# Attention and MLP kernel, front of the program: the first query tile on SyncE's queue, a scan and a memset behind the first sums, two row loads behind the bias rows

## The chip, the cores and the metric

The kernel runs on one core of one Trainium2 chip. The metric is device time in microseconds (us); the time before is the median of 3 runs, 344.49 us (343.03 to 345.12). Engine names: TensorE (PE), VectorE (DVE), ScalarE (ACT), GpSimd (POOL), SyncE (SP). SyncE, ScalarE and GpSimd issue DMA transfers; each executes its own instructions in order.

## The reference

Selective attention over 8 batches, 8 heads, 576 positions and 64 channels per head, and then a layer norm with a two-layer MLP on the 512 joined channels:

```python
scores = (q @ k.T) / sqrt(64)
cum = cumsum(maximum(s, 0))                       # along the positions
bias = -(cum[:, None] - cum[None, :])
scores = where(causal, -1e9, scores + minimum(bias, 0))
x = softmax(scores) @ v                           # heads joined: [8, 576, 512]
out = x + maximum(layernorm(x, g) @ w1, 0) @ w2   # w1 [512, 2048], w2 [2048, 512]
```

Inputs and output are float32. The matrix products run in bfloat16.

## The kernel before

The program runs once through the eight batches; the attention of a batch overlaps the MLP of an earlier one. Weights w1 and w2 are kept in SBUF. Nothing loops at run time: the order of the work is a list of step names, PLAN, written out by hand as one long string and run through by the loop at the end of `fast_path`, which looks each name up in STEPS. Each engine gets its instructions in the order of that list, and a step on one engine waits for its inputs by semaphores.

The bias is not added to the scores. The cumulative sums c of s (64 rows, one for each batch and head, by 576 positions) are split into three bfloat16 parts (high, middle, low), and these stand as four more rows below the 64 channels of q and k, so that the score product of 68 rows contains the bias. For batch 0 the parts go in as columns beside the loaded q and k rows (tile `rowb`, 128 positions at a time), and TensorE transposes the whole tile; for batch 1 they go in by small DMAs of rows (`aug`, lines 262 to 267, four transfers on SyncE for each half of the heads).

What happens at the front, with the names of the steps:

- Loads ahead of PLAN (lines 900 to 965): SyncE loads the first 256 positions of s (`c_first`), the first k tile (`ld_tile`, float32) and the rest of s (`c_in`); ScalarE's queue loads the first q tile. GpSimd issues all the loads that cast to bfloat16, in a fixed order: k and q tiles 1 and 2, v tiles, w1 pieces, the pairs `kp` and `qp`, the last k and q tile (64 positions), and later the five v tiles of batch 1 (line 192), w1 and w2.
- `relu.0` and `relur.1`, `relur.2`: relu and scale of the three stretches of s (0 to 128, 128 to 256, 256 to 576), the first on VectorE, the others on ScalarE. `scan.0`, `scan.1`, `scan.2` (line 293, VectorE): their cumulative sums, each started from the last column of the one before.
- `hi`, `sub`, `mid`, `lo` (lines 307 to 312): the three parts of a stretch; for stretch 0 all on VectorE, for the others the casts `hi` and `mid` on ScalarE. `tc` transposes the parts on TensorE, `bc` (lines 282 and 286, VectorE) puts them into `rowb`.
- `cq` and `ck.0` (line 141, ScalarE): casts of the loaded first q and k tile into `rowb`.
- `m` (line 1257, VectorE): memset of the rows of `rowb` behind the last 64 positions, and of a small constant for the layer norm.
- `W.n`: n matmuls on zeros (line 889, 512 columns each) that keep TensorE at work.
- `T.t.g` (line 978) transposes tile t for the heads of group g (four heads, 8 transposes), `e` evacuates it to `kq`, `S` and `x` are its scores and exponentials, `V.t.g` (line 1058) its product with v.
- `lr.3.0` (`ld_rows`, line 206): two float32 loads on SyncE, the first 128 positions of batch 3's k and q, into two tiles of the pool `stage` of 8. Their reader is `cr.3.0.0` (line 218, a cast on GpSimd), much later in PLAN.
- `aug` writes batch 1's bias rows for the first half of its heads into `kq[2]`; it waits for the parts of c and for GpSimd's memset of `kq[2]` (line 941).
- `v.8` (line 590) is the first product of batch 1 with its v tiles, five key blocks.

Of the kernel before, what the change touches and what calls it, by code (L numbers as in the profile page):

```python
# [30 lines left out]
def fast_path(  # L31
# [12 lines left out]
    nc = tc.nc  # L44
    B, H, S, D = q.shape
# [115 lines left out]
    def tile_src(kind, t):  # L161
        pn = P if t < NF else TL
        src = k if kind == "k" else q
        return src[0, :, t * P : t * P + pn, :].rearrange("h s d -> s h d")
# [6 lines left out]
    def ld_tile(kind, t, eng):  # L171
        tmp = stage.tile([P, H, D], F32, name="tiletmp", tag="st")
        eng.dma_start(out=tmp, in_=tile_src(kind, t))
        loaded[kind, t] = tmp
# [723 lines left out]
    )  # L898
    s_rows = s.rearrange("b h s -> (b h) s")
    nc.sync.dma_start(out=c_first, in_=s_rows[:, 0 : 2 * P])  # L900
    ld_tile("q", 0, nc.scalar)
    ld_tile("k", 0, nc.sync)
    nc.sync.dma_start(out=c_in[:, 2 * P : S], in_=s_rows[:, 2 * P : S])

    nc.vector.memset(zeros.bitcast(F32), 0.0)
# [315 lines left out]
    def raise_flag(count, ones, n):  # L1221
# [97 lines left out]
    }  # L1319

    PLAN = """
        relu.0 scan.0 relur.1 O cq hi.0 scan.1 ck.0 sub.0 mid.0 lo.0 m hi.1 tc.0 bc.0 sub.1 W.2 T.0.1 relur.2
        mid.1 scan.2 e.0.1:A lo.1 T.0.0 W.1 hi.2 tc.1 S.0.1.0 bc.1 T.1.0 e.0.0:A sub.2 T.1.1 S.0.0.0 qu.1 mid.2
        x.0.1.0 lo.2 V.0.1 tc.2 e.1.0:A e.1.1:D S.1.1.1 x.0.0.0 x.1.1.1 qu.2 S.1.0.0 V.0.0 N.0.1 S.1.1.0 bc.2
        T.2.0 N.0.0 x.1.1.0 T.2.1 e.2.0:D S.1.0.1 lr.3.0 lp.9 V.1.1 x.1.0.1 S.2.0.1 e.2.1:D S.2.0.2 S.2.1.2
        T.3.0 S.2.1.1 N.1.1 S.2.0.0 B.0.1 L.0 x.1.0.0 V.1.0 x.2.0.1 x.2.0.2 x.2.1.2 X.0 e.3.0:D N.1.0 x.2.1.1
        L.1 x.2.0.0 S.2.1.0 S.3.0.2 T.3.1 B.1.0 x.2.1.0 e.3.1:D B.1.1 S.3.0.0 S.3.0.3 y.0:A aug x.3.0.2 V.2.0
        M.0.0.0 x.3.0.3 M.0.0.3 S.3.0.1 V.2.1 S.3.1.1 x.3.0.1 N.2.0 M.0.0.2 bc.4 S.3.1.3 x.3.0.0 X.1 y.1:A
        x.3.1.3 N.2.1 M.0.0.1 S.3.1.2 V.3.0 L.2 T.4.0 S.3.1.0 M.0.1.0 r.0.0:A M.0.1.3 N.3.0 X.2 x.3.1.2 Q.q.4
        x.3.1.0 x.3.1.1 e.4.0:D T.4.1 y.2:D M.0.1.2 Q.k.4 E.q.4.0:A B.3.0 E.k.4.0:A S.4.0.1 e.4.1:D S.4.1.0  # L1330
# [253 lines left out]
def kernel(tc, q, k, v, s, g, w1, w2, out):  # L1584
    nc = tc.nc
    with tc.tile_pool(name="flag", bufs=1) as pool:
        flag = pool.tile([1, 1], I32, name="flag")
        bad = fast_path(tc, q, k, v, s, g, w1, w2, out, flag)
        with tc.If(bad > 0):
            general_path(tc, q, k, v, s, g, w1, w2, out)  # L1590
# [28 lines left out]
```

## Time and profile before

| | |
|---|---|
| median of 3 runs | 344.49 us (343.03 to 345.12) |
| the profiled execution's own time | 344.98 us |
| its span, first to last instruction | 343.4 us |
| TensorE clock granted, mean | 0.997 |
| ScalarE, VectorE, GpSimd busy | 186.5, 201.4, 167.3 us |
| moved by DMA | 48.59 MB, 147962 packets |

Times in the profile's rows are us from the start of the span. In a row of a timeline the first number is the start and the second the duration; instructions that follow each other at one line are merged (x8 is eight of them, and the duration is that from the first start to the last end). The bracket tells how long the engine was idle ahead of the row and what ended that: `[0.30 <-DMA rowb<-in_k_dram]` is 0.30 us of waiting for a load of k into `rowb`. `SPq` and `ACTq` rows are DMA issues, not the transfers; a DMA row in the chain of waits runs from the issue to the landing. The rows of DMA queues give packets, MB and the time that the packets took as a share of 16 engines' time in that window.

### The profile page before, as it was taken

Reading aid. Unit: us, or ns where it says so; the run is one execution under the profiler, and the core shown is the slowest. Engines: PE = TensorE matmul, PEld = TensorE weight load, DVE = VectorE, ACT = ScalarE, POOL = GpSimd, SP = SyncE. Lnnn points to the kernel's source line nnn. Section 1 sums busy time; section 2 is a strip of 40 time slices with the busy share of each in tenths; the row PEclk is TensorE's granted clock in tenths of the full one; section 3 lists DMA queues with packets and bytes.
Section 4 is the critical chain, followed back from the end, with each engine's and each line's share of the span. In section 5 each row is a group of like instructions: output and inputs, shape, how many; then the busy total and the mean of one; then the engine's idle time right before and its main releaser. Section 6 shows DMA issues by size and latency. Waiting matters only on the chain.

```text
span 343.4 us, 8036 instructions
## 1 busy us (share of the span) xinstructions
PE 330.9 (96%) x3093; PEld 183.1 (53%) x3117; DVE 201.4 (59%) x568; ACT 186.5 (54%) x347; POOL 167.3 (49%) x305
## 2 busy tenths in 40 slices
PE   7999999999999899999999999999999999999994
PEld 2899765555455455545555545554455444444443
DVE  6688787946586577457643664566448624533412
ACT  4888999678655676457636764487344204202200
POOL 8897678886579762884774376431301001000000
PEclk9999999999999999999999999999999999999998
DMA  9999999899999999999987966700510141021022
GB/s 145 181 190 181 204 196 207 193 227 227 194 206 211 205 211 187 213 222 219 208 184 193 216 109 148 139 2 2 122 63 2 30 123 46 3 84 38 3 62 65
DMA packets 147962, 48.59 MB, mean 141 GB/s; under 512 B 135280, under 2 KB 143760, under 8 KB 147920
## 3 DMA queue, kind: packets, MB, share of 16 engines
q1 hardware_dynamic: 121856, 38.34, 54.5%
q0 software_dynamic: 24304, 8.92, 22.2%
q10 hardware_dynamic: 1760, 0.79, 1.0%
q8 instruction: 25, 0.41, 0.5%
q14 instruction: 17, 0.14, 0.1%
HBM read 37.11 MB, written 9.44 MB: 136 GB/s over the span
## 4 chain that ended last, share of the span: by engine, by line
PE 71%; POOL 11%; DMA 9%; issue 2%; SPq 2%; DVE 2%; ACT 1%; POOLq 0%; ACTq 0%
PE py L811 30%; PE ph L792 29%; DMA v_bf<-in_v_dram 5%; PE pot L626 3%; DMA kq<-rowb 2%; SPq L206 2%; PE sa L553 2%; POOL er L497 2%; POOL v_bf L192 1%; DMA rowtmp<-in_q_dram 1%; POOL v_bf L233 1%; ACT er L560 1%; PE pott L664 1%; PE sb L553 1%; PE pot L590 1%
## 5 line engine op out<-in xcount | busy, mean ns | idle before, releaser
L811 PE MATMUL py<-w_bf,hT 128*128 128x512 bf16 (+2 forms) x584 | 128.8, 367 | 1.8 <-issue 0.6
L792 PE MATMUL ph<-xT,w_bf 128*128 128x512 bf16 x480 | 110.0, 379 | 0.9 <-DMA xT<-xn 0.9
L783 ACT ACTIVATE hT<-ph 128x512 bf16<-128x512 f32 x102 | 61.0, 605 | 80.7 <-PE ph L792 79.0
L811 PEld LDWEIGHTS <-hT 128*128 128x128 bf16 x608 | 56.0, 98 | 60.2 <-issue 0.2
L792 PEld LDWEIGHTS <-w_bf 128*128 128x128 bf16 x544 | 51.2, 98 | 57.3 <-DMA xT<-xn 1.4
L497 POOL TENSOR_SCALAR_AFFINE_SELECT er<-er 128x256 bf16<-128x256 bf16 x96 | 37.9, 411 | 50.7 <-ACT er L560 36.3
L823 DVE SCALAR_TENSOR_TENSOR yo<-py,rstd,xb 128x512 f32<-128x512 f32 x32 | 24.0, 751 | 49.1 <-PE py L811 44.6
L560 ACT ACTIVATE er<-sb 128x512 bf16<-128x512 f32 x48 | 28.2, 609 | 21.0 <-PE sb L553 21.0
L781 DVE TENSOR_SCALAR hT<-ph 128x512 bf16<-128x512 f32 x34 | 23.4, 691 | 27.2 <-PE ph L792 25.2
L560 ACT ACTIVATE er<-sa 128x512 bf16<-128x512 f32 x48 | 28.6, 609 | 15.1 <-PE sa L553 14.8
L233 POOL TENSOR_TENSOR v_bf<-rowtmp,wt 128x512 bf16<-128x512 f32 (+1 forms) x30 | 32.2, 1081 | 2.6 <-DMA rowtmp<-in_v_dram 2.4
L560 ACT ACTIVATE er<-sc 128x512 bf16<-128x512 f32 x48 | 28.8, 613 | 5.3 <-PE sc L553 5.3
L715 POOL TENSOR_TENSOR rstd<-rstd,mhalf 128x4 f32<-128x4 f32 (+1 forms) x8 | 8.8, 1094 | 34.7 <-DVE rstd L714 33.2
L741 DVE SCALAR_TENSOR_TENSOR xn<-xb,mv,gb 128x512 bf16<-128x512 f32 x28 | 25.0, 894 | 1.0
L218 POOL CAST kq<-rowtmp 128x512 bf16<-128x512 f32 (+1 forms) x30 | 18.5, 626 | 13.7 <-DMA rowtmp<-in_k_dram 13.0
L626 PEld LDWEIGHTS <-er 128*128 128x128 bf16 x480 | 19.7, 97 | 10.0 <-POOL er L497 1.3
L643 DVE TENSOR_REDUCE sums<-pot 128x4 f32<-128x8 f32 x48 | 7.8, 162 | 29.2 <-PE pot L626 29.1
L700 DVE BATCH_NORM_STATS2 stats<-xb 128x6 f32<-128x128 f32 (+1 forms) x84 | 24.6, 326 | 0.6
L626 PE MATMUL pot<-v_bf,er 128*128 128x66 bf16 x480 | 22.1, 193 | 0.3 <-POOL er L497 0.2
L645 DVE TENSOR_TENSOR xb<-pot,rinvs 128x256 f32<-128x256 f32 x48 | 20.4, 425 | 1.7
L553 PEld LDWEIGHTS <-kq 64*128 64x128 bf16 x384 | 12.0, 94 | 9.7 <-issue 4.0
L218 POOL CAST rowb<-rowtmp 128x512 bf16<-128x512 f32 (+1 forms) x20 | 13.8, 696 | 1.9 <-DMA rowtmp<-in_k_dram 1.0
(178 smaller groups left out, 394.9 us busy)
## 6 DMA issues: line engine op xcount, KB each, us to landing
out_dram<-yo SPq DMA_DIRECT2D x32, 256.0 KB
rowtmp<-in_v_dram SPq DMA_DIRECT2D x24, 256.0 KB
rowtmp<-in_k_dram SPq DMA_DIRECT2D x20, 256.0 KB
rowtmp<-in_q_dram SPq DMA_DIRECT2D x20, 256.0 KB
w_bf<-in_moe_w_ch_dram POOLq DMA_DIRECT2D x8, 512.0 KB, 9.1
kp<-in_k_dram POOLq DMA_DIRECT2D x8, 144.0 KB, 8.9
qp<-in_q_dram POOLq DMA_DIRECT2D x8, 144.0 KB, 9.0
v_bf<-in_v_dram POOLq DMA_DIRECT2D x8, 128.0 KB, 8.1
```

What stands on the lines that cost most here:

```text
L218: nc.gpsimd.tensor_copy(out=rows[b % 2][0:pn, t, u], in_=loaded.pop(("kq"[u], b, t))[0:pn])
L233: e.tensor_tensor(out=v_bf[b % 2][0:pn, t, :, 0:D], in0=loaded.pop(("v", b, t))[0:pn], in1=wt[0:pn, t, b, :].unsqueeze(2).to_broadcast([pn ...
L497: nc.gpsimd.affine_select(out=out, in_=out, compare_op=ALU.is_ge, fill=0.0, base=0, pattern=pattern, channel_multiplier=-1,)
L560: nc.scalar.activation(out=er[:, 2 * n % 4 + i, o : o + 512], in_=bank["B", n].pop((name, i)), func=ACT.Exp, scale=scale,)
L626: nc.tensor.matmul(pot[:, t, :], lhsT=e[:, o : o + P], rhs=v_bf[b % 2][:, kb, h, :], start=(kb == 0), stop=(kb == t),)
L700: nc.vector.bn_stats(out=st[b][:, t, part, :], in_=x_tiles(b)[t][:, lo:hi])
L741: nc.vector.scalar_tensor_tensor(out=xn, in0=tiles[t], scalar=mvs[b][:, t, 0:1] if b > 0 else mean0[:, t : t + 1], in1=gb, op0=ALU.subtrac ...
L781: nc.vector.tensor_scalar_max(out=dst, in0=ph, scalar1=0.0)
L783: nc.scalar.activation(out=dst, in_=ph, func=ACT.Relu)
L792: nc.tensor.matmul(ph, lhsT=w1_bf[:, kd, fb * P : (fb + 1) * P], rhs=xT[:, :, kd, :], start=(kd == 0), stop=(kd == KD - 1),)
L811: nc.tensor.matmul(py[t], lhsT=hT[:, fb, t * P : (t + 1) * P], rhs=w2_bf[:, fb, c0:c1], start=(fb == 0), stop=(fb == FB - 1),)
L823: nc.vector.scalar_tensor_tensor(out=yo, in0=py[t], scalar=rs, in1=x[:, c0:c1], op0=ALU.mult, op1=ALU.add)
```

## The change

Three edits at the front; no instruction's arithmetic changes.

1. The first q tile is loaded on SyncE's queue, behind the first k tile and ahead of the rest of s, instead of on ScalarE's queue.
2. In PLAN `scan.1` goes from behind `hi.0` to behind `lo.0`, and `m` from behind `lo.0` to behind `sub.1`; `ck.0` comes ahead of `cq` on ScalarE, and both keep their place ahead of `hi.1`; `W.2` ahead of the first tile's transposes becomes `W.1`.
3. `lr.3.0` goes from behind `S.1.0.1` to behind `aug`; its two loads thus stand behind `aug`'s four on SyncE's queue.

```diff
     nc.sync.dma_start(out=c_first, in_=s_rows[:, 0 : 2 * P])
-    ld_tile("q", 0, nc.scalar)
     ld_tile("k", 0, nc.sync)
+    ld_tile("q", 0, nc.sync)
     nc.sync.dma_start(out=c_in[:, 2 * P : S], in_=s_rows[:, 2 * P : S])
...
     PLAN = """
-        relu.0 scan.0 relur.1 O cq hi.0 scan.1 ck.0 sub.0 mid.0 lo.0 m hi.1 tc.0 bc.0 sub.1 W.2 T.0.1 relur.2
+        relu.0 scan.0 relur.1 O ck.0 hi.0 sub.0 mid.0 lo.0 scan.1 cq hi.1 tc.0 bc.0 sub.1 m W.1 T.0.1 relur.2
...
-        T.2.0 N.0.0 x.1.1.0 T.2.1 e.2.0:D S.1.0.1 lr.3.0 lp.9 V.1.1 x.1.0.1 S.2.0.1 e.2.1:D S.2.0.2 S.2.1.2
...
+        T.2.0 N.0.0 x.1.1.0 T.2.1 e.2.0:D S.1.0.1 lp.9 V.1.1 x.1.0.1 S.2.0.1 e.2.1:D S.2.0.2 S.2.1.2 T.3.0
...
+        x.2.0.0 S.2.1.0 S.3.0.2 T.3.1 B.1.0 x.2.1.0 e.3.1:D B.1.1 S.3.0.0 S.3.0.3 y.0:A aug lr.3.0 x.3.0.2 V.2.0
```

The lines of PLAN between are only wrapped anew.

More of the change, by code (lines that the diff above doesn't have):

```diff
@@ L1321, in fast_path @@
     PLAN = """
-        relu.0 scan.0 relur.1 O cq hi.0 scan.1 ck.0 sub.0 mid.0 lo.0 m hi.1 tc.0 bc.0 sub.1 W.2 T.0.1 relur.2
+        relu.0 scan.0 relur.1 O ck.0 hi.0 sub.0 mid.0 lo.0 scan.1 cq hi.1 tc.0 bc.0 sub.1 m W.1 T.0.1 relur.2
         mid.1 scan.2 e.0.1:A lo.1 T.0.0 W.1 hi.2 tc.1 S.0.1.0 bc.1 T.1.0 e.0.0:A sub.2 T.1.1 S.0.0.0 qu.1 mid.2
         x.0.1.0 lo.2 V.0.1 tc.2 e.1.0:A e.1.1:D S.1.1.1 x.0.0.0 x.1.1.1 qu.2 S.1.0.0 V.0.0 N.0.1 S.1.1.0 bc.2
-        T.2.0 N.0.0 x.1.1.0 T.2.1 e.2.0:D S.1.0.1 lr.3.0 lp.9 V.1.1 x.1.0.1 S.2.0.1 e.2.1:D S.2.0.2 S.2.1.2
-        T.3.0 S.2.1.1 N.1.1 S.2.0.0 B.0.1 L.0 x.1.0.0 V.1.0 x.2.0.1 x.2.0.2 x.2.1.2 X.0 e.3.0:D N.1.0 x.2.1.1
-        L.1 x.2.0.0 S.2.1.0 S.3.0.2 T.3.1 B.1.0 x.2.1.0 e.3.1:D B.1.1 S.3.0.0 S.3.0.3 y.0:A aug x.3.0.2 V.2.0
+        T.2.0 N.0.0 x.1.1.0 T.2.1 e.2.0:D S.1.0.1 lp.9 V.1.1 x.1.0.1 S.2.0.1 e.2.1:D S.2.0.2 S.2.1.2 T.3.0
+        S.2.1.1 N.1.1 S.2.0.0 B.0.1 L.0 x.1.0.0 V.1.0 x.2.0.1 x.2.0.2 x.2.1.2 X.0 e.3.0:D N.1.0 x.2.1.1 L.1
+        x.2.0.0 S.2.1.0 S.3.0.2 T.3.1 B.1.0 x.2.1.0 e.3.1:D B.1.1 S.3.0.0 S.3.0.3 y.0:A aug lr.3.0 x.3.0.2 V.2.0
         M.0.0.0 x.3.0.3 M.0.0.3 S.3.0.1 V.2.1 S.3.1.1 x.3.0.1 N.2.0 M.0.0.2 bc.4 S.3.1.3 x.3.0.0 X.1 y.1:A
```

## Prediction

> **What bounds the kernel now.** I read the page first, for the engine that carries the span.
>
> ```profile
> span 343.4 us, 8036 instructions
> PE 330.9 (96%) x3093; PEld 183.1 (53%) x3117; DVE 201.4 (59%) x568; ACT 186.5 (54%) x347; POOL 167.3 (49%) x305
> DMA  9999999899999999999987966700510141021022
> PE 71%; POOL 11%; DMA 9%; issue 2%; SPq 2%; DVE 2%; ACT 1%; POOLq 0%; ACTq 0%
> ```
>
> TensorE is busy for 96% of the span, and the DMA engines are at nine tenths or more for its first half. All the edits lie in the first 20 us, so next comes the chain of waits, in order of time, up to the place where TensorE takes it over.
>
> ```profile
> 3.77 7.71 DMA v_bf<-in_v_dram
> ...
> 28.25 8.01 DMA v_bf<-in_v_dram
> ...
> 36.30 0.19 PE pot L590
> ```
>
> The end is not set by the bias sums at the front. It is set by the row of casting loads that GpSimd issues, down to the last tile of batch 1's v, issued at 28.25 and landed at 36.26; the first attention product of batch 1 (step v.8) stands there. From 36.3 the chain is nearly all TensorE. The timeline of TensorE shows the same from its side: its waits in this stretch, with their releasers in brackets.
>
> ```profile
> 7.08 1.05 PE L889 MATMUL idle<-hT 128*128 128x512 bf16 x2
> 8.00 1.89 PE L978 MATMUL trt<-ident,rowb 128*68 128x128 bf16 x16
> 10.83 1.17 PE L978 MATMUL trt<-ident,rowb 128*68 128x128 bf16 x16
> 23.14 0.64 PE L1058 MATMUL pot<-v_bf,er 128*128 128x65 bf16 x16
> 24.08 0.36 PE L978 MATMUL trt<-ident,rowb 96*68 96x96 bf16 x4 [0.30 <-DMA rowb<-in_k_dram]
> 24.66 0.36 PE L978 MATMUL trt<-ident,rowb 96*68 96x96 bf16 x4 [0.22 <-DMA rowb<-in_q_dram]
> 26.07 0.50 PE L978 MATMUL trt<-ident,rowb 96*68 96x96 bf16 x8
> 35.94 0.55 PE L590 MATMUL pot<-v_bf,er 128*128 128x65 bf16 x6 [0.38 <-DMA v_bf<-in_v_dram]
> ```
>
> Three waits, all for casting loads: 0.30 and 0.22 us for the last k and q tile of batch 0, 0.38 us for batch 1's v. So two questions decide: how much earlier TensorE comes to v.8, and whether that v lands earlier or later.
>
> **Part 1: the sums (scan, memset, warm-up).** The timelines of VectorE and ScalarE:
>
> ```profile
> 5.67 0.47 DVE L293 TENSOR_TENSOR_SCAN c_sc<-c_one,c_sc,hT 64x128 f32<-64x128 f32 x1
> 6.07 0.26 DVE L312 TENSOR_TENSOR hT<-c_sc,c 64x128 f32<-64x128 f32 x1
> ...
> 6.67 0.28 DVE L312 TENSOR_TENSOR c<-hT,c 64x128 bf16<-64x128 f32 x1
> 7.13 0.51 DVE L1257 MEMSET rowb<- 32x544 uint32 x1 [0.17 <-issue]
> 7.67 0.18 DVE L282 COPY rowb<-trc 128x24 bf16<-128x24 bf16 x1
> ```
>
> Today the second scan (5.67 to 6.07, start to start) lies between the first high part and its rest, and the memset (7.13 to 7.67) between the last low part and the bias columns. Taken out, they give 0.40 + 0.54 us; the scan comes back behind the low part, ahead of the columns, at its 0.40 to 0.47. The columns also need the third transpose, about 0.3 us behind the low part, which then runs beside the scan. So the columns can start near 7.67 - 0.40 - 0.54 + 0.43 = 7.2, and the tile transposes near 7.5 instead of 8.00: 0.5 us. The memset costs nothing later: its rows are read by the transposes at 24.08. One warm-up matmul of two goes; both took 1.05 us, and with the columns 0.5 us sooner one fits ahead of them.
>
> **Part 2: the first q tile moves from ScalarE's queue to SyncE's, behind k.** ScalarE's rows are the ones that wait on these loads:
>
> ```profile
> 4.61 0.31 ACT L1260 ACTIVATE hT<-hT 64x128 f32<-64x128 f32 x1 [1.59 <-DMA hT<-in_s_dram]
> 4.84 0.62 ACT L141 CAST rowb<-tiletmp 128x512 bf16<-128x512 f32 x1
> 5.84 0.62 ACT L141 CAST rowb<-tiletmp 128x512 bf16<-128x512 f32 x1 [0.38 <-DMA tiletmp<-in_k_dram]
> ...
> 7.11 0.47 ACT L1260 ACTIVATE c_in<-c_in 64x320 f32<-64x320 f32 x1 [0.45 <-DMA c_in<-in_s_dram]
> ...
> 9.07 1.01 ACT L141 COPY kq<-trt 68x1024 bf16<-68x1024 bf16 x1 [0.64 <-PE trt L978]
> ```
>
> q is cast at 4.84 without a wait, k at 5.84, as soon as it lands. The ScalarE issue that goes (0.44 us) frees an engine that waits for s until 4.61 anyway: nothing. What counts is the DMA; its queues by window (q10 is ScalarE's queue, q1 SyncE's, q0 GpSimd's), 2 to 3 and 4 to 5 us:
>
> ```profile
> DMA packets 499, 0.13 MB, mean 129 GB/s; under 512 B 498, under 2 KB 499, under 8 KB 499
> q10 hardware_dynamic: 498, 0.13, 55.1%
> q1 hardware_dynamic: 1, 0.00, 0.3%
> ...
> q1 hardware_dynamic: 671, 0.17, 100.1%
> ```
>
> Before 3 us only ScalarE's queue moves data, 0.13 MB of it; SyncE's starts at 3. After the change nothing moves before 3, and s, k, q and the rest of s follow each other in one queue. At 0.17 MB/us the first 0.32 MB (s, k) are through near 4.9, so k lands somewhat sooner than 5.84; q's 0.26 MB take 1.5 us at that rate, 2.1 at the rate beside casting loads below (0.12), so q lands at 6.4 to 7.0 and is cast by 7.0 to 7.6; the rest of s lands at 7.6 to 8.0 instead of 7.11. This is the new wait: behind the q cast ScalarE holds the second high part, the relu of the rest of s, a middle part and the first evacuation (9.07 now), and VectorE's second rest, memset and third scan wait for those. I take 8.7 for that evacuation (8.4 to 9.0): front gain 0.4 us of the 0.5.
>
> **Part 3: batch 3's first k and q rows go behind batch 1's bias rows on SyncE.** Four windows price it: 6 to 10, 10 to 14, 25 to 29 and 43 to 46 us.
>
> ```profile
> q0 software_dynamic: 2055, 0.26, 100.4%
> q1 hardware_dynamic: 1964, 0.49, 72.5%
> ...
> q0 software_dynamic: 4867, 0.62, 249.2%
> ...
> q0 software_dynamic: 967, 0.80, 127.2%
> ...
> q0 software_dynamic: 495, 0.45, 89.7%
> q1 hardware_dynamic: 486, 0.12, 31.3%
> ```
>
> From 6 to 10 the casting loads move 0.26 MB beside SyncE's 0.49; from 10 to 14, alone, 0.62. Without the two row loads (0.52 MB) they gain 0.62 - 0.26 = 0.36 MB, 2.3 us at 0.155 MB/us. Against it stands the lost start: 0.13 MB, 0.7 us at the 0.19 MB/us of 6 to 10. So the casting loads run about 1.6 us ahead, and GpSimd's two waits for landings in its own issue go:
>
> ```profile
> 11.76 0.75 POOL L253 DMA_DIRECT2D w_bf<-in_moe_w_ch_dram  x1 [0.46 <-DMA v_bf<-in_v_dram]
> ...
> 14.41 0.64 POOL L184 DMA_DIRECT2D qp<-in_q_dram  x1 [0.27 <-DMA v_bf<-in_v_dram]
> ...
> 17.17 0.76 SPq L265 DMA_DIRECT2D kq<-c  x1
> 17.98 1.95 SPq L267 DMA_DIRECT2D kq<-c  x3
> ...
> 40.83 0.63 POOL L218 CAST kq<-rowtmp 128x512 bf16<-128x512 f32 x1
> ```
>
> The last k and q tiles of batch 0 then land before TensorE asks. From the end of 23.14's row (23.78) to 24.86 the eight transposes took 1.08 us against 0.50 at 26.07: gain 0.6. TensorE would reach v.8's waiting block 0.4 + 0.6 = 1.0 us sooner, at 34.6 instead of 35.56 (35.94 less 0.38).
>
> But the 0.52 MB come back. The four bias-row issues that they are moved past run to 19.93 now, some 0.7 sooner after, and the two issues follow; nothing stands behind them on SyncE until the next bias rows. The bias rows moved no packet before 21, some 4 us after issue, so I let the row data begin at 23.3. Beside large casting packets they go at 0.12/3 = 0.04 MB/us and slow the casting loads from 0.80/4 = 0.20 to 0.45/3 = 0.15, a quarter: six us to 29.3, cost 1.5. The rest, 0.28 MB, meets batch 1's v, in packets as small as from 6 to 10: 0.12 MB/us, 2.3 us at 58% loss, cost 1.3. All is in by 31.6, well ahead of its only reader, GpSimd's cast at 40.83, so that wait is nothing; after 40.83 each us late would hold GpSimd's queue of loads and masks. Sum for the v tiles: 2.8 - 1.6 = 1.2 us later. The other end is that bytes are conserved and the lost start is refilled: 0, or -0.6 if a third of the row data trails v. I take +0.6, the middle of 0 and 1.2.
>
> In the window from 43 to 46 the two queues moved 495 and 486 packets. The Trainium skill, DMA: Bandwidth & Descriptors, Queues, rings and completion order, says that each DMA engine takes turns between its queues by packet; the trace agrees. By turns with large packets all the way the row loads would take 13 us (0.52 MB at 0.04), and the casting loads would lose a quarter of that, 3.2 us: v 1.6 us later instead of my 1.2.
>
> **The sum.** TensorE's 1.0 us is lost at v.8, which waits for v at 36.26 + 0.6; nothing behind it is shortened, so the wait there grows from 0.38 to about 2 us. The profiled execution took 344.98 us (span 343.4), 0.5 above the median of 344.49. Its own sum is 345.6; against the median 345.1, and I say 345.0. About 1% (3.4 us) is what a measurement of this kernel can tell from no change.
>
> **Rivals.** (a) Faster: the row data trails behind v, because SyncE's queue stays slow. Then v lands 1.6 us sooner, TensorE arrives at 34.6, and at most 0.38 + 1.0 = 1.4 us are gained: 343.1. For it: 0.04 MB/us from 43 to 46. Against: v comes in small packets. Decides when v's last tile lands before 36.0. Chance 0.22.
>
> (b) Slower: GpSimd's issue pace (a load each 0.9 us), not the shared bandwidth, holds the casting loads early, so nothing runs ahead and the 2.8 us plus 0.7 lost start are paid whole: v at 39.7, 348.0. Against: the first v tile, issued at 3.77, lands 7.7 us later, so many loads lie queued. Decides when v lands behind 38. Chance 0.14.
>
> (c) TensorE stays at its early pace: 16 transposes took 1.89 us at 8.00 and 1.17 at 10.83. If the slow pace lasts longer, so that the work of 10.3 to 13.7 takes twice as long, TensorE comes to v.8 at 35.56 - 1.0 + 3.4 = 38.0, 1.7 behind today's 36.3: 346.2. Chance 0.09. The Trainium skill, TensorE: Matmul & The Clock Gate, Part 1, says that full rate takes about 3.4 us of sustained work; the row of warm-up and transposes from 7.08 to 9.9 agrees in size, though the granted clock shows full speed throughout. It speaks against the warm-up matmul that goes; by it the slow stretch would be 3.4 us of time, a loss of 1.7 us, which the wait at v.8 hides.
>
> (d) No effect at all: 344.5, chance 0.08 beside the forecast's 0.42; unseen 0.05.
>
> **How the numbers follow.** Forecast 345.0, own range 343.9 to 346.2 (v between -0.6 and +1.2). The range 342.6 to 347.4 takes in (a) and (c) with the 1.5 us by which single runs stray below the median, and leaves out (b)'s upper half and the unseen. Slower by over 1% (above 347.9): half of (b), 0.07, and 0.03 of the unseen: 0.10. Faster by over 1% (below 341.1): no mechanism reaches it; 0.02 of the unseen and 0.02 for (a) on a low run: 0.04. Within 1%: 0.86.
>
> **What would show it.** Right: the first evacuation near 8.7, no wait for k or q tiles near 24, TensorE at v.8 near 34.6 and a wait there of 1 to 3 us ending between 36.0 and 37.5, SyncE's queue at work from 23 to 32. Wrong: v landing before 35.5 or after 38, GpSimd waiting for row data at 40, or a half-paced TensorE after 11 us.

## The result, and the profile after

| | before | after |
|---|---|---|
| median of 15 runs each, side by side | 344.71 us (342.93 to 347.17) | 346.97 us (344.53 to 349.83) |
| ratio, 95% interval | 1 | 1.0053 (1.0030 to 1.0076) |
| the profiled execution's own time | 344.98 us | 348.22 us |

The change makes the kernel 0.5% slower, some 1.8 us of 344.7. That is less than the 1% that the prediction took for what one measurement can tell from no change, but the interval over 15 runs excludes zero. The ratios here and below leave out runs more than 1.5% above the fastest of their kernel (two of the 15 of after, three of the ten of "the rows alone" and two of the twelve of "the q tile and the order", the profiled ones of these two kernels among them), while the medians are over all runs, so that a quotient of two medians can differ from the ratio. The profiled execution of after is 1.25 us above its median, and so the two profiles differ by 3.2 us, more than the kernels do. What is read in them has to be weighed with that in mind.

The page of the kernel after: engines, the granted clock in 40 slices, the moved bytes, the chain's shares.

```profile
span 346.6 us, 8033 instructions
PE 331.6 (96%) x3092; PEld 184.5 (53%) x3116; DVE 204.4 (59%) x568; ACT 186.1 (54%) x347; POOL 166.8 (48%) x305
...
PEclk9699999999999999999999999999999999999999
...
PE 85%; DVE 7%; issue 3%; DMA 2%; ACT 1%; POOL 1%; SPq 0%; POOLq 0%
```

TensorE still carries the span. DMA has fallen from 9% of the chain of waits to 2%, and GpSimd from 11% to 1%: the chain no longer runs along the casting loads. The second slice of the clock, 8.7 to 17.3 us, shows 6 where before showed 9. The chain of waits of after says what took the loads' place.

```profile
2.31 5.43 DMA tiletmp<-in_q_dram
...
7.76 0.62 ACT rowb L141
...
11.82 1.71 PE trt L978 x16
...
37.34 0.46 PE pot L590 x15
```

It begins with the q tile that moved, goes over its cast to TensorE, and stays with TensorE from 10.7 on. At v.8 there is no landing in it: the block of 15 products runs through without a stop and ends at 37.80, where before the last one, held by v, ended at 36.30 + 0.19 = 36.49. So TensorE comes out of v.8 1.3 us later, and not because it waited there. Nor was v late. The first row is the issue of batch 1's five v tiles, the second the last and smallest of them, with the us from issue to landing at its end:

```profile
23.70 4.24 POOL L192 DMA_DIRECT2D v_bf<-in_v_dram  x5
...
v_bf<-in_v_dram POOLq DMA_DIRECT2D x1, 64.0 KB, 8.8
```

Issued at 27.18, it landed at 36.0, 0.2 us sooner than in before (36.26). What is late is TensorE. Its timeline in after:

```profile
6.24 0.38 PE L978 MATMUL trt<-ident,rowb 128*68 128x128 bf16 x4 [0.16 <-DVE rowb L286]
8.43 1.11 PE L978 MATMUL trt<-ident,rowb 128*68 128x128 bf16 x12 [1.81 <-ACT rowb L141]
...
11.61 1.91 PE L978 MATMUL trt<-ident,rowb 128*68 128x128 bf16 x16
...
26.11 0.51 PE L978 MATMUL trt<-ident,rowb 96*68 96x96 bf16 x8
...
37.18 0.62 PE L590 MATMUL pot<-v_bf,er 128*128 128x65 bf16 x15
```

The transposes start at 6.24 instead of 8.00, but only the four of k; then TensorE waits 1.81 us for the cast of q. The next sixteen take 1.91 us where the row of before at 10.83 took 1.17. The last eight of batch 0, at 26.11, have no wait in front of them. ScalarE and VectorE of after show the wait's origin:

```profile
3.36 0.31 ACT L1260 ACTIVATE hT<-hT 64x128 f32<-64x128 f32 x1 [0.82 <-DMA hT<-in_s_dram]
5.17 0.62 ACT L141 CAST rowb<-tiletmp 128x512 bf16<-128x512 f32 x1 [1.50 <-DMA tiletmp<-in_k_dram]
7.76 0.62 ACT L141 CAST rowb<-tiletmp 128x512 bf16<-128x512 f32 x1 [1.97 <-DMA tiletmp<-in_q_dram]
...
9.21 1.00 ACT L141 COPY kq<-trt 68x1024 bf16<-68x1024 bf16 x1
```

```profile
5.51 0.47 DVE L293 TENSOR_TENSOR_SCAN c_sc<-c_one,c_sc,hT 64x128 f32<-64x128 f32 x1
5.91 0.18 DVE L282 COPY rowb<-trc 128x24 bf16<-128x24 bf16 x1
...
8.61 0.28 DVE L312 TENSOR_TENSOR hT<-c_sc,c 64x128 f32<-64x128 f32 x1 [2.43 <-ACT c L307]
```

The bias columns are in at 5.91 (before 7.67), and q comes at 7.76. The first evacuation, at 9.21, is 0.14 later than before's 9.07. What the wait did to TensorE's pace stands in the windows of after; the columns are window and length, busy time and count of PE, PEld, DVE, ACT and POOL, the granted clock, the DMA share and GB/s.

```profile
8.00:10.00 2.00, 1.57 (x15) 1.21 (x15) 1.19 (x4) 1.93 (x5) 2.00 (x3) 0.72 2.43 155
10.00:12.00 2.00, 1.42 (x15) 1.30 (x14) 1.29 (x5) 1.71 (x4) 2.00 (x4) 0.50 2.43 155
12.00:14.00 2.00, 2.00 (x22) 2.00 (x21) 0.92 (x2) 1.72 (x3) 1.97 (x3) 0.50 1.72 206
14.00:16.00 2.00, 2.00 (x26) 1.74 (x25) 1.21 (x6) 0.60 (x1) 1.99 (x2) 0.57 1.61 182
16.00:18.00 2.00, 2.00 (x42) 2.00 (x40) 1.28 (x5) 1.19 (x2) 2.00 (x4) 1.00 1.59 187
```

The granted clock is at half through the windows from 10 to 14 and comes back before 16: this execution lost the early gain in that slow stretch. The other load that moved, the row data, shows in the DMA queues of after, in the windows 6 to 10 and 25 to 29, and in the cast that reads it:

```profile
q0 software_dynamic: 4319, 0.55, 213.5%
q1 hardware_dynamic: 212, 0.11, 13.5%
...
q0 software_dynamic: 761, 0.65, 104.4%
q1 hardware_dynamic: 742, 0.19, 24.2%
```

```profile
40.57 0.63 POOL L218 CAST kq<-rowtmp 128x512 bf16<-128x512 f32 x1
```

Early the casting loads now move 0.55 MB where they moved 0.26, and from 25 to 29 they move 0.65 where they moved 0.80, beside 0.19 MB on SyncE's queue. The cast waits for nothing.

Most of the rest of the 3.2 us between the two profiles lies in the layer norm, which the change doesn't touch. The first two rows are from the timelines of VectorE and TensorE in after, the third the summed waits of TensorE in after (us, times, longest); the last is the same view of before.

```profile
100.42 5.03 DVE L741 SCALAR_TENSOR_TENSOR xn<-xb,mv,gb 128x512 bf16<-128x512 f32 x1
...
107.42 1.89 PE L811 MATMUL py<-w_bf,hT 128*128 128x512 bf16 x7 [1.62 <-DVE yo L823]
```

```profile
PE py L811 <- DVE yo L823: 2.6, 3, 1.6
```

```profile
PE ph L792 <- DMA xT<-xn: 0.9, 1, 0.9
```

One VectorE instruction of the layer norm takes 5.03 us there, and TensorE then waits 1.62 us for VectorE. Two more such waits, 0.59 us at 66.98 and 0.41 us at 72.03, stand behind another long one (2.52 us at 63.43; 1.97 us in before). The profiles of "the q tile alone" and "less warm-up" below have these two as well, with the row loads in their old place, so they are not the moved rows' doing. Before had none of the three waits, but one of 0.9 us for a transfer that is gone in after. 1.3 + 2.6 - 0.9 = 3.0 of the 3.2 us.

### The profile page after: what moved, and what is told of

Its sections match the earlier page's. It is cut to its first block, busy times and chain, and to the rows that moved or that the text cites. A ratio compares the mean times of both kernels' runs of the same rounds, so it can differ in the third digit from the quotient of the medians.

```text
span 346.6 us, 8033 instructions
## 1 busy us (share of the span) xinstructions
PE 331.6 (96%) x3092; PEld 184.5 (53%) x3116; DVE 204.4 (59%) x568; ACT 186.1 (54%) x347; POOL 166.8 (48%) x305
## 4 chain that ended last, share of the span: by engine, by line
PE 85%; DVE 7%; issue 3%; DMA 2%; ACT 1%; POOL 1%; SPq 0%; POOLq 0%
PE ph L792 33%; PE py L811 31%; PE pot L626 4%; DVE xn L741 3%; PE ph L1102 2%; PE sa L553 2%; PE st L1000 2%; DMA tiletmp<-in_q_dram 2%; PE pott L664 1%; PE sb L553 1%; PE sc L553 1%; PE pot L590 1%; PE trt L978 1%; PE pot L1058 1%; DVE yo L823 1%
## 5 line engine op out<-in xcount | busy, mean ns | idle before, releaser
L741 DVE SCALAR_TENSOR_TENSOR xn<-xb,mv,gb 128x512 bf16<-128x512 f32 x28 | 29.3, 1048 | 1.0
L1017 ACT ACTIVATE er<-st 128x512 bf16<-128x512 f32 x24 | 13.1, 607 | 3.0 <-PE st L1008 2.9
```

The lines of the kernel that those rows point to most:

```text
L741: nc.vector.scalar_tensor_tensor(out=xn, in0=tiles[t], scalar=mvs[b][:, t, 0:1] if b > 0 else mean0[:, t : t + 1], in1=gb, op0=ALU.subtrac ...
```

## The experiments

Two theories stood against each other. By the one the rows cost it: their 0.52 MB go ahead of batch 1's v, v is late at v.8, and that is the loss. By the other the q tile costs it: TensorE's wait for q drops its clock. Both can hold, so the three edits were first taken apart. The ratios are against before on the same chip, from 6 to 12 runs of each kernel and 23 to 33 of before. A profile is one execution; where it lies far from its kernel's median, its own time is given.

**The change with q back on ScalarE's queue.**

```diff
+    ld_tile("q", 0, nc.scalar)
     ld_tile("k", 0, nc.sync)
-    ld_tile("q", 0, nc.sync)
```

> The changed kernel with the first query tile loaded on ScalarE's queue again, ahead of k; the other two edits stay. Theory A (the late q tile: in the changed kernel it landed at 7.74 instead of before 4.84, TensorE stood still for 1.81 us in the middle of the first tile's transposes, and the granted clock fell to 0.5 from 8.9 to 15.7): the loss of 0.5% goes, ratio to the kernel before 0.995 to 1.000, no wait of TensorE between 6.2 and 8.4, full clock from about 9 to 10.5 on, batch 1's first product begun by 35. Rival B (the row loads behind the bias rows delay the casting loads): ratio stays at 1.003 to 1.008 and the last v tile of batch 1 lands behind 36.3. Rival C (the new order of the sums, and one warm-up matmul less): ratio stays at 1.003 to 1.008 with a low clock behind 10.5.

Median 344.95, ratio 1.0031 (1.0000 to 1.0063). The mean granted clock over its runs is 0.995, as for before, where after has 0.990. The profiled execution took 349.12 us, the longest of the twelve. TensorE's timeline:

```profile
34.55 0.22 PE L590 MATMUL pot<-v_bf,er 128*128 128x65 bf16 x2 [0.25 <-DMA v_bf<-in_v_dram]
35.89 0.25 PE L590 MATMUL pot<-v_bf,er 128*128 128x65 bf16 x3 [1.11 <-DMA v_bf<-in_v_dram]
36.60 0.28 PE L590 MATMUL pot<-v_bf,er 128*128 128x65 bf16 x4 [0.47 <-DMA v_bf<-in_v_dram]
37.06 0.53 PE L590 MATMUL pot<-v_bf,er 128*128 128x65 bf16 x6 [0.18 <-DMA v_bf<-in_v_dram]
```

This is the forecast's picture: without the wait for q TensorE arrives at 34.55 and then loses 2.01 us in four waits for v, the last until 37.06. In the stretch behind, the granted clock fell:

```profile
37.00:38.00 1.00, 0.93 (x15) 0.80 (x15) 0.34 (x2) 0.00 (x0) 0.90 (x2) 0.64 1.25 205
38.00:39.00 1.00, 1.00 (x4) 0.30 (x2) 0.97 (x3) 0.60 (x1) 1.00 (x3) 0.50 1.22 198
```

So waits at v.8 cost twice: their own length, and in this execution a stretch at half pace. Taking the q edit back removes the half pace between 10 and 14 (16 transposes at 10.19 took 1.05 us), and the estimate falls from 1.0053 to 1.0031; the intervals overlap.

**The q tile alone**, on the kernel before:

```diff
-    ld_tile("q", 0, nc.scalar)
     ld_tile("k", 0, nc.sync)
+    ld_tile("q", 0, nc.sync)
```

> The kernel before with only the query tile moved to SyncE's queue, behind k. Theory A: it carries the whole loss, ratio 1.004 to 1.010; with the old order of the sums the q tile is cast at 7.7, and because the second high part stands behind it on ScalarE, the first evacuation comes at 9.1 or later; the row loads still stand in front, so the casting loads land no sooner than before and the wait at v.8 does not hide more. Rivals B and C: ratio 0.998 to 1.002.

Median 345.28, ratio 1.0027 (0.9995 to 1.0059), mean clock 0.995. TensorE's timeline has the wait, and all sixteen transposes behind it at 1.08 us, full pace:

```profile
8.33 1.08 PE L978 MATMUL trt<-ident,rowb 128*68 128x128 bf16 x16 [1.59 <-ACT rowb L141]
```

The transposes start 0.33 us later than before's and take 1.08 us instead of 1.89. No loss is shown.

**The order of the front alone** (only PLAN's first line, as in the change's diff).

```diff
-        relu.0 scan.0 relur.1 O cq hi.0 scan.1 ck.0 sub.0 mid.0 lo.0 m hi.1 tc.0 bc.0 sub.1 W.2 T.0.1 relur.2
+        relu.0 scan.0 relur.1 O ck.0 hi.0 sub.0 mid.0 lo.0 scan.1 cq hi.1 tc.0 bc.0 sub.1 m W.1 T.0.1 relur.2
```

> The kernel before with only the first line of the list of steps from the changed one (scan and memset behind the chain of the first sums, k cast ahead of q, one warm-up matmul less). Theory A: no loss, ratio 0.997 to 1.001; the bias columns come 0.5 us sooner, 7.2 instead of 7.67, but the gain is lost at v.8, which waits for v until about 36.2 as before. Rival C: ratio 1.003 to 1.008, and a clock of 0.5 behind 10.5 us.

Median 344.84, ratio 1.0013 (0.9976 to 1.0050). The transposes start at 7.20:

```profile
7.20 1.05 PE L978 MATMUL trt<-ident,rowb 128*68 128x128 bf16 x16 [0.16 <-ACT rowb L141]
```

The reorder brings TensorE 0.8 us sooner to its transposes, more than the 0.5 of the forecast. It reaches v.8 at 34.35 (before: 35.13), and its last product there is held by v until 35.25. It leaves v.8 at 35.44, 1.05 us ahead of before, because the same v tiles landed that much sooner in this execution (343.91 us). In the median the gain is not seen.

**The rows alone.**

```diff
-        T.2.0 N.0.0 x.1.1.0 T.2.1 e.2.0:D S.1.0.1 lr.3.0 lp.9 V.1.1 x.1.0.1 S.2.0.1 e.2.1:D S.2.0.2 S.2.1.2
+        T.2.0 N.0.0 x.1.1.0 T.2.1 e.2.0:D S.1.0.1 lp.9 V.1.1 x.1.0.1 S.2.0.1 e.2.1:D S.2.0.2 S.2.1.2
...
-        L.1 x.2.0.0 S.2.1.0 S.3.0.2 T.3.1 B.1.0 x.2.1.0 e.3.1:D B.1.1 S.3.0.0 S.3.0.3 y.0:A aug x.3.0.2 V.2.0
+        L.1 x.2.0.0 S.2.1.0 S.3.0.2 T.3.1 B.1.0 x.2.1.0 e.3.1:D B.1.1 S.3.0.0 S.3.0.3 y.0:A aug lr.3.0 x.3.0.2 V.2.0
```

> The kernel before with only the two row loads of batch 3 moved behind the bias rows. Theory A: ratio 0.996 to 1.001; the casting loads land 1.5 to 2 us sooner up to 22 us, TensorE's waits for the last k and q tile at 24.08 and 24.66 go, and v of batch 1 lands between 35.5 and 36.5. Rival B: v of batch 1 lands at 36.9 to 37.5 and the ratio is 1.002 to 1.005.

Median 346.98, ratio 1.0039 (0.9998 to 1.0079): the largest of the three parts, though its interval just touches no change. In the profiled execution (349.02 us) the chain of waits runs over the last v tile, which lands 2.6 us behind before's:

```profile
27.79 11.04 DMA v_bf<-in_v_dram
...
38.87 0.19 PE pot L590
```

**The whole change with TensorE kept at work during the wait for q**: eight more matmuls on zeros between the k half and the q half of the first transposes. They are added work, made to keep the clock.

```diff
+            if (t, g, u) == (0, 1, 1):
+                keep_warm(8)
```

> The changed kernel with eight more matmuls on zeros between the k half and the q half of the first tile's transposes, where TensorE stood still for 1.81 us. The wait for the q tile stays; only the idle time is filled. Over all runs the mean granted clock of the changed kernel is 0.9896 (15 runs) and that of the kernel before 0.9953 (33 runs): about 1.2 stretches at half clock more per run, each worth 1.7 us of TensorE. Theory A1 (the idle time costs by the clock): mean clock back to 0.994 to 0.996 and ratio to the kernel before 1.000 to 1.004. Rival A2 (the late q tile costs by the wait itself, the clock is a bystander): ratio stays at 1.004 to 1.008, whatever the clock. Theory D (half of the loss is the row loads in front of batch 1's v, as the first four runs hint: rows alone 1.0039, q alone 1.0027, order alone 1.0013): what stays is 1.002 to 1.004.

Median 346.54, ratio 1.0028 (0.9996 to 1.0061). The mean clock goes from 0.990 to 0.997: the stretch at half pace is gone. In its place TensorE waits at v.8 again, 0.78 us in the timeline of the profiled execution (343.48 us, the shortest of the twelve):

```profile
36.07 0.56 PE L590 MATMUL pot<-v_bf,er 128*128 128x65 bf16 x6 [0.78 <-DMA v_bf<-in_v_dram]
```

The estimate is half of the change's 0.0053, but the two intervals overlap; the share of the lost clock isn't settled by this.

**The q tile and the order, rows left in front.** The edits of the second and third experiment together.

```diff
-    ld_tile("q", 0, nc.scalar)
     ld_tile("k", 0, nc.sync)
+    ld_tile("q", 0, nc.sync)
...
-        relu.0 scan.0 relur.1 O cq hi.0 scan.1 ck.0 sub.0 mid.0 lo.0 m hi.1 tc.0 bc.0 sub.1 W.2 T.0.1 relur.2
+        relu.0 scan.0 relur.1 O ck.0 hi.0 sub.0 mid.0 lo.0 scan.1 cq hi.1 tc.0 bc.0 sub.1 m W.1 T.0.1 relur.2
```

> The kernel before with the q tile on SyncE and the new order of the sums, the row loads still in front. Theory A1: the k half of the first transposes runs early, TensorE then waits for q, so the mean clock falls to 0.989 to 0.992 although neither edit alone lowered it (0.9950 and 0.9953); ratio 1.003 to 1.007. Theory D alone (the row loads carry the loss): clock near 0.995, ratio 0.999 to 1.003.

Median 346.18 against 345.17 of before in that session, ratio 1.0010 (0.9980 to 1.0041), with a mean clock of 0.989. The low clock of after is here in full, and the moved rows are not: on average the time is not measurably off. That doesn't make the half pace free. Of the ten runs in the ratio, the four with a mean clock of 0.988 or less took 346.6 us on average, the other six 344.8; in after it is 347.4 us (six runs) and 346.0 (seven). Which of the two, clock or time, follows from the other, these numbers don't tell. In the profiled execution (349.03 us, the longest) TensorE comes to v.8 at 39.01, behind a half clock from 10 to 20, and doesn't wait there.

**The rows behind v.** The kernel before, with the row loads behind batch 1's second bias rows, and their cast moved to the cast of the second rows.

```diff
-        T.2.0 N.0.0 x.1.1.0 T.2.1 e.2.0:D S.1.0.1 lr.3.0 lp.9 V.1.1 x.1.0.1 S.2.0.1 e.2.1:D S.2.0.2 S.2.1.2
+        T.2.0 N.0.0 x.1.1.0 T.2.1 e.2.0:D S.1.0.1 lp.9 V.1.1 x.1.0.1 S.2.0.1 e.2.1:D S.2.0.2 S.2.1.2
...
-        B.0.0 U xk cr.3.0.0 a3 lr.3.1 Q.k.6 E.k.5.1:A x.4.1.1 E.k.6.0:A u V.4.1 s.9 E.k.6.1:D N.4.1 V.4.0 Q.q.6
+        B.0.0 U xk a3 lr.3.0 lr.3.1 Q.k.6 E.k.5.1:A x.4.1.1 E.k.6.0:A u V.4.1 s.9 E.k.6.1:D N.4.1 V.4.0 Q.q.6
...
-        E.q.7.1:D wT v.11 lp.10 u wx n.11 lv.2.0 A.0 u d.14 ga.1.0.0 v.12 qu.4 n.12 O2.k.9:A s.14 cr.3.1.0
+        E.q.7.1:D wT v.11 lp.10 u wx n.11 lv.2.0 A.0 u d.14 ga.1.0.0 v.12 qu.4 n.12 O2.k.9:A s.14 cr.3.0.0 cr.3.1.0
```

> The kernel before with the two row loads issued still later: behind the second set of bias rows, so that their data run behind batch 1's v; their reader on GpSimd moves with them, ahead of its next cast. Theory D (the 0.52 MB beside or ahead of v set v's landing): v's last tile lands by 35, the wait at v.8 is under 0.4 us, ratio 0.994 to 0.999, and against the rows directly behind the first bias rows (1.0039) 0.5% or more better. Rival E (v's landing is set by the slowest of the DMA engines, whatever stands ahead of it): v lands between 35.5 and 38.5 as in all runs so far, ratio 0.998 to 1.004. Loss possible where batch 3's rows come too late: then the first batch-3 transposes would hold GpSimd and TensorE near 90 us.

Median 351.07, ratio 1.0161 (1.0134 to 1.0187). Two rows of its timeline, the first product at v.8 and GpSimd's cast of the rows, and what TensorE waits for then:

```profile
34.22 0.62 PE L590 MATMUL pot<-v_bf,er 128*128 128x65 bf16 x15
```

```profile
59.67 0.61 POOL L218 CAST kq<-rowtmp 128x512 bf16<-128x512 f32 x1 [6.14 <-DMA rowtmp<-in_k_dram]
...
61.73 1.09 PE L590 MATMUL pot<-v_bf,er 128*128 128x65 bf16 x15 [5.25 <-POOL er L411]
```

The half that speaks to the theory of the rows came out: with them out of the way v.8 runs without a wait, from 34.22, and ends at 34.84 instead of 36.49. But GpSimd, in order, then stands 6.14 us in front of its cast, the masks behind it are late, and TensorE waits 5.25 us. The time of this kernel measures that wait, not the rows' effect on v.

**The same with the new order of the front.** The edits of the kernel just told (left out here), and those of "the order of the front alone".

```diff
-        relu.0 scan.0 relur.1 O cq hi.0 scan.1 ck.0 sub.0 mid.0 lo.0 m hi.1 tc.0 bc.0 sub.1 W.2 T.0.1 relur.2
+        relu.0 scan.0 relur.1 O ck.0 hi.0 sub.0 mid.0 lo.0 scan.1 cq hi.1 tc.0 bc.0 sub.1 m W.1 T.0.1 relur.2
```

> The same with the new order of the sums as well (q tile still on ScalarE's queue): the version that should be best by Theories A1 and D, since the early bias columns are then not lost to a wait for v: ratio 0.991 to 0.998. Rival E: 0.998 to 1.004.

Median 351.36, ratio 1.0171 (1.0139 to 1.0202). The same loss; the order's gain can't show behind it.

**The q tile and the rows, old order.** The edits of "the q tile alone" and "the rows alone"; those of the rows are left out here.

```diff
-    ld_tile("q", 0, nc.scalar)
     ld_tile("k", 0, nc.sync)
+    ld_tile("q", 0, nc.sync)
...
```

> The kernel before with the q tile on SyncE and the row loads behind the bias rows, but the old order of the sums with its two warm-up matmuls. So far all kernels with the rows moved lay at 1.0028 to 1.0053 and those without at 1.001 to 1.0027; the mean clock fell to 0.989 only where q and the new order came together. Theory D (the row loads carry the loss): ratio 1.003 to 1.005. Theory A1 (q with the new order carries it, by the clock): mean clock 0.994 to 0.996 here and ratio 1.000 to 1.003.

Median 346.34, ratio 1.0051 (1.0014 to 1.0089): as much as the whole change. The order of the front is not needed for the loss. The profiled execution took 346.30 us, and in it v is no more waited for than in after: the block at v.8 runs through from 36.23 to 36.85, 0.4 us behind before's end, with a half clock from 10 to 13 ahead of it (16 transposes at 11.19 took 1.91 us).

**The rows doubled.** All four row loads of batch 3's first two tiles in front of v; `lr.3.0` is taken from its old place as in "the rows alone" (left out here).

```diff
...
-        L.1 x.2.0.0 S.2.1.0 S.3.0.2 T.3.1 B.1.0 x.2.1.0 e.3.1:D B.1.1 S.3.0.0 S.3.0.3 y.0:A aug x.3.0.2 V.2.0
+        L.1 x.2.0.0 S.2.1.0 S.3.0.2 T.3.1 B.1.0 x.2.1.0 e.3.1:D B.1.1 S.3.0.0 S.3.0.3 y.0:A aug lr.3.0 lr.3.1 x.3.0.2 V.2.0
...
-        B.0.0 U xk cr.3.0.0 a3 lr.3.1 Q.k.6 E.k.5.1:A x.4.1.1 E.k.6.0:A u V.4.1 s.9 E.k.6.1:D N.4.1 V.4.0 Q.q.6
+        B.0.0 U xk cr.3.0.0 a3 Q.k.6 E.k.5.1:A x.4.1.1 E.k.6.0:A u V.4.1 s.9 E.k.6.1:D N.4.1 V.4.0 Q.q.6
```

> The kernel before with four row loads behind the first bias rows instead of two: the next tile of batch 3's k and q, which stood behind the second bias rows, comes there too, so 1.05 MB run ahead of batch 1's v. Theory D: v's last tile lands 2 to 4 us later than in the kernel before (36.26), at 38.5 to 40.5; TensorE's wait at v.8 grows to 3 us or more and the clock falls once behind it; ratio 1.003 to 1.010, less than in proportion where the later loads of SyncE, now freed of 0.52 MB, give some back. Rival E (v's landing is set by the slowest DMA engine and not by the bytes ahead): v lands between 35 and 38.9 as in the runs so far, ratio as with two loads, 1.002 to 1.005.

Median 350.75, ratio 1.0184 (1.0151 to 1.0216). TensorE's timeline at v.8, and two windows behind it:

```profile
34.62 0.22 PE L590 MATMUL pot<-v_bf,er 128*128 128x65 bf16 x2 [0.28 <-DMA v_bf<-in_v_dram]
36.54 0.25 PE L590 MATMUL pot<-v_bf,er 128*128 128x65 bf16 x3 [1.70 <-DMA v_bf<-in_v_dram]
37.97 0.38 PE L590 MATMUL pot<-v_bf,er 128*128 128x65 bf16 x4 [1.18 <-DMA v_bf<-in_v_dram]
39.65 0.51 PE L590 MATMUL pot<-v_bf,er 128*128 128x65 bf16 x6 [1.30 <-DMA v_bf<-in_v_dram]
```

```profile
38.00:40.00 2.00, 0.69 (x11) 0.58 (x11) 0.00 (x0) 0.00 (x0) 0.63 (x1) 0.50 1.40 200
40.00:42.00 2.00, 2.00 (x15) 0.99 (x13) 1.34 (x4) 0.60 (x1) 1.83 (x3) 0.50 1.24 206
```

Nothing ahead of v.8 but the row loads was moved in this kernel, and yet it loses 6.4 us, more than any theory expected. The four waits for v add up to 4.46 us, and the clock is at half behind them. This is the one run on the rows that stands clear of the noise: more row data ahead of v, later v, a longer wait, a longer time. It shows the direction, and not the price of half as much data.

**Less warm-up at the front.** The kernel before with one matmul on zeros ahead of PLAN instead of nine, and none in its first lines, so that TensorE's half pace lasts longer with all loads as they were.

```diff
-    keep_warm(9)
+    keep_warm(1)
...
-        relu.0 scan.0 relur.1 O cq hi.0 scan.1 ck.0 sub.0 mid.0 lo.0 m hi.1 tc.0 bc.0 sub.1 W.2 T.0.1 relur.2
-        mid.1 scan.2 e.0.1:A lo.1 T.0.0 W.1 hi.2 tc.1 S.0.1.0 bc.1 T.1.0 e.0.0:A sub.2 T.1.1 S.0.0.0 qu.1 mid.2
+        relu.0 scan.0 relur.1 O cq hi.0 scan.1 ck.0 sub.0 mid.0 lo.0 m hi.1 tc.0 bc.0 sub.1 T.0.1 relur.2
+        mid.1 scan.2 e.0.1:A lo.1 T.0.0 hi.2 tc.1 S.0.1.0 bc.1 T.1.0 e.0.0:A sub.2 T.1.1 S.0.0.0 qu.1 mid.2
```

> The kernel before with hardly any warm-up: 1 matmul on zeros in place of the first 9, and none in place of the two and the one between the first steps. It prices the half clock by itself. Theory S (the wait at v.8 covers a late TensorE): mean clock 0.986 to 0.992, ratio 0.999 to 1.003, v.8 begun 1 to 2 us later than at 35.1 but its wait for v gone. Theory A1 (each stretch at half clock costs its 1.7 us): ratio 1.004 to 1.008.

Median 345.04, ratio 1.0017 (0.9990 to 1.0045). Its block at v.8 starts at 35.39, against 35.13 in before, and runs through in 0.81 us, 0.2 more than without any stop:

```profile
35.39 0.81 PE L590 MATMUL pot<-v_bf,er 128*128 128x65 bf16 x15
```

A slower front costs 0.6 us by the estimate, and possibly nothing: at v.8 the wait took it in, for the block ends at 36.20, before's at 36.49. The mean clock over the runs is 0.999 where 0.986 to 0.992 was expected, although 16 transposes at 7.79 took 1.89 us and 16 at 10.76 took 1.91, half pace: the profile shows a clock of 1.00 in all windows from 6 to 14. So a mean clock leaves the first slow stretch out, here and in before.

**The rows late, their cast later still.** The new order of the front, the row loads behind those of batch 3's third tile, and both casts of their halves moved to just ahead of the transposes that read them, so that GpSimd need not stand. This was the candidate to beat both kernels. The lines with the old places of `lr.3.0` and its casts and the first line of PLAN are left out here.

```diff
...
-        v.15 O2.q.8:A O2.q.9:A U n.15 F.q.9 qu.6 lr.3.2 O2.k.11:A vo.2:P u ga.1.2.0 ga.1.2.1 ga.1.0.1 La.2 me
+        v.15 O2.q.8:A O2.q.9:A U n.15 F.q.9 qu.6 lr.3.2 lr.3.0 O2.k.11:A vo.2:P u ga.1.2.0 ga.1.2.1 ga.1.0.1 La.2 me
...
-        cr.3.3.0 bx.9.0 Y.8.0 cr.3.3.1 K.8.0 tr.3.0.2 cr.3.4.1 K.8.1 bm.9.3 bx.9.2 bm.9.0 bx.9.3 bx.9.1 bm.9.1 u
+        cr.3.3.0 bx.9.0 Y.8.0 cr.3.3.1 K.8.0 cr.3.0.0 cr.3.0.1 tr.3.0.2 cr.3.4.1 K.8.1 bm.9.3 bx.9.2 bm.9.0 bx.9.3 bx.9.1 bm.9.1 u
```

> A try at a better version: the new order of the sums, q on ScalarE's queue, and the two row loads as late as batch 3 allows, behind that batch's third tile, with both their casts on GpSimd just ahead of the first batch-3 transposes. Theory D: v lands by 35, TensorE is 1 to 1.5 us ahead at 52 as with the rows behind v, and GpSimd is not held by a row cast at 53 to 60; ratio 0.994 to 0.999. It loses where SyncE's queue can't bring batch 2's v and batch 3's rows in time: then TensorE waits for GpSimd between 70 and 95 and the ratio is 1.000 to 1.010.

Median 344.51 against 344.34, ratio 1.0001 (0.9977 to 1.0026). v.8 runs from 33.92 without a wait and ends at 34.54, 1.9 us ahead of before. Most of this lead goes to the edit itself, near 77: GpSimd waits 0.81 us for q's rows ahead of its casts at 74.29, its masks behind them are late, and TensorE waits for these twice.

```profile
PE pot L626 <- POOL er L497: 1.1, 2, 0.7
```

At 78.33 the lead is 0.4 us (the score products that start there start at 78.71 in before). The rest is gone by 104 us: VectorE's instruction of the layer norm takes 5.30 us, and TensorE waits 1.9 us for VectorE once.

```profile
96.79 5.30 DVE L741 SCALAR_TENSOR_TENSOR xn<-xb,mv,gb 128x512 bf16<-128x512 f32 x1
```

No version ran measurably faster than the kernel before.

**Taken together.** The five kernels with the rows behind the first bias rows have 1.0031, 1.0039, 1.0028, 1.0051 and 1.0053, on average 1.0040. The three with the rows in front and one or both of the other edits have 1.0027, 1.0013 and 1.0010, on average 1.0017. The difference is 0.0023, 0.8 us; the rows alone against before gave 0.0039, 1.3 us. Each kernel's own interval is about as wide as these effects (0.3 to 0.4% to each side), so the split is an estimate. What is shown clear of the noise is the direction, by the doubled rows. And the two readings don't meet: by the averages the moved rows carry most of the loss, but in the profiles of after and of "the q tile and the rows", which move both the rows and q, TensorE waits for no v and the half pace stands in its place.

## Why the prediction was right or wrong, point by point

- **The direction and the range** held: no gain, within 1% of before, a little to the slow side. The size didn't: the sum was +0.6 us against its own profile, and +1.8 us were measured, past the forecast's own range of 343.9 to 346.2. The path didn't either: in after's profile TensorE comes late to v.8 and waits for nothing there, and one of the signs that the prediction named for being wrong is seen, a half-paced TensorE after 11 us. That the time still fell within the wide range is in part luck.
- **What bounds the front: the casting loads down to batch 1's v, so that a gain ahead of v.8 is lost there.** Borne out only where q keeps its old queue, and in one execution: the change with q on its old queue arrived at v.8 at 34.55, the forecast's 34.6, and waited 2.01 us, the forecast's "about 2 us", in the longest of its twelve runs. The new order alone saved 0.8 us at the first transposes, and over the runs no gain is seen; in its profile, though, v came 1.05 us sooner than in before and the lead was not lost at v.8. In after itself that wait is not there, for the next reason.
- **"Front gain 0.4 us of the 0.5"** failed. The term was a q cast by 7.0 to 7.6 and an evacuation at 8.7. The cast ran from 7.76 to 8.38, and the evacuation began at 9.21. The part on the sums was too small in the other direction: the columns came at 5.91, not 7.2, which fits that s came sooner with no q beside it (ScalarE's relu of s began at 3.36 and not 4.61). Earlier columns and a later q left TensorE 1.81 us without work in the middle of its transposes. I priced that as lateness of one evacuation, 0.4 us of gain left over; the profile shows in its place a half clock until almost 16 and TensorE at v.8 at 37.18 instead of 34.6.
- **Rival (c), the half-paced TensorE,** named this way of going wrong, with v.8 reached at 38.0 and a time of 346.2, at a chance of 0.09. The profiled execution follows it, at 37.18. I tied it to the warm-up matmul that goes. The agreement in size that I read in the row from 7.08 to 9.9 is doubtful: TensorE had worked from 1.49 to 5.51 before it (nine matmuls in 4.02 us) and was still at half pace at 8.00. The runs point to the wait for q together with the new order: the order alone, which drops that matmul, and q alone both keep a mean clock of 0.995, as before; q and order together have 0.989. What the half pace costs isn't settled: with it and without the moved rows the ratio is 1.0010 (0.9980 to 1.0041), but within that kernel the runs of lower clock are 1.7 us longer.
- **"Sum for the v tiles: 1.2 us later... I take +0.6"** is a term that after's profile doesn't show: there v's last tile landed at 36.0, 0.2 us sooner than in before. Its parts held: the casting loads ran ahead early (0.55 MB from 6 to 10, I said up to 0.62), the last eight transposes of batch 0 had no wait, the row data moved at 0.19 / 4 = 0.05 MB/us and slowed the casting loads from 0.20 to 0.16, where I had 0.04 and 0.15. With q back on its queue v let TensorE go on at 37.06, where it did so at 35.94 in before: 1.1 us. With the rows alone the last product came 2.6 us later than in before, and over the runs the rows cost 0.8 to 1.3 us by the estimates. So a single landing strays by more than the term, and its size stays open. Beside that the sum had no price for the clock: waits at v.8 of 2 us or more in sum were followed by half pace with q back on ScalarE, with the rows alone and with the rows doubled. "Nothing behind it is shortened" was true, but something behind it was lengthened.
- **Rival (a), the row data trails v:** not seen. The kernels that made it true by the order (rows behind v, rows late) did bring v.8 from 36.49 to an end at 34.84 and 34.54, as that rival says; the gain didn't reach the end. **Rival (b), v behind 38:** 38.87 in the profile of the rows alone and 39.65 with doubled rows, but not in after.
- **Row data late for its reader: nothing.** Right, the cast at 40.57 didn't wait. The bound given, that each us late beyond it holds GpSimd, came out dear in the rows behind v: 6.14 us of waiting, and 5.9 us of time in the medians.

**What stays open.** How the change's 1.8 us divide between the rows, the clock and the waits in the layer norm: the kernel with the fill, which keeps the clock, and the one with q and the order, which leaves the rows in front, both have intervals that overlap with that of the change. Why the last v tile comes at times up to two us apart in kernels with the rows in the same place (the last product at v.8 at 35.25 in the order alone, 36.30 in before, 37.12 in q alone). Each of these loads gives sixteen signals as its parts land, and the kept traces show that the last parts stray and not the first: for the last v tile they run from 32.92 to 36.26 in before, from 33.60 to 36.02 in after, from 33.58 to 37.34 with q back and from 33.26 to 38.83 in the rows alone. What holds the last parts isn't known. And whether the stall near 100 us belongs to the change: it stands in the one profile each of four kernels, and of these the late rows and the order alone have ratios of 1.0001 and 1.0013, so it does not make a kernel slow by itself.

## What to carry to other kernels

Where two streams join, here TensorE's work and the loads that feed v.8, a gain on the stream that waits is worth nothing, and data put ahead of the late stream's last load can be paid: 6.4 us for 1.05 MB here, where the waits for v were 4.5 us and the clock fell to half behind them, and about 1 us for 0.52 MB by an estimate that the noise nearly covers. When a load moves behind another in a queue, ask not only when its reader starts but what TensorE does in the gap, since a pause in work that was continuous can be followed by half pace. And hold a profiled execution against the median of its runs before its waits are added up.

## What the runs showed of the hardware

- **TensorE's clock can fall after pauses shorter than two us, and the length of one pause doesn't decide.** The wait of 1.81 us for q in after and the one of 1.69 us in the q tile and the rows were followed by a half granted clock (16 transposes took 1.91 us, at 11.61 and at 11.19). So was one of 1.36 us in the q tile and the order, with two more of 0.48 and 0.69 us behind it (1.91 us at 11.64). The one of 1.59 us in the q tile alone was not (eight transposes took 0.61 us at 10.56), nor were those of 1.79 us near 103 in the order alone and of 1.89 us near 104 with late rows. What does decide, these six can't tell. The Trainium skill, TensorE: Matmul & The Clock Gate, HAM oscillation — how this bites in real kernels, has the rule that there should be no idle gaps of TensorE above about 3.4 us; these runs show half pace after gaps half as long.
- **The granted clock isn't the whole story at the start.** In before, 16 transposes at 8.00 took 1.89 us while the record shows full speed from 6 on; in after, 16 at 11.61 took 1.91 us and the record shows 0.50. The pace of equal rows tells the state where the record does not, and a mean clock near 1 does not exclude a slow start.
- **One VectorE instruction stretched sixfold.** The layer norm's xn (28 of them, median 0.752 us) took 5.03 us once in after (and 2.52 us at 63.43), 4.77 with q back, 4.98 in the order alone and 5.30 with late rows, in after and with late rows with GpSimd's casts, products and masks back to back beside it. The Trainium skill, SBUF — State Buffer, SBUF: two separate sides, says that a VectorE operation with two SBUF inputs and a GpSimd one that reads SBUF share a port pair as an exclusive lock: whichever starts first has it for the whole instruction, and the other is blocked. The rows agree in kind, though 5 us is several GpSimd instructions long. No run took GpSimd's work away there, so this cause is argued and not shown.
